# An adaLN block on one Trainium2 core: SyncE's transfers in the MLP phase in the order of the source, and several of them in other half steps

## The chip, the core and the metric

The kernel runs on one core of a Trainium2 chip (trn2). It is one program with one launch. The metric is the device time of one execution in microseconds (us); where several runs are told, their median is given. The profile is one profiled execution of the same program, with a time of its own.

The engines are named as the profile names them: PE is TensorE's matmuls and PEld its weight loads, DVE is VectorE, ACT is ScalarE, POOL is GpSimd and SP is SyncE. SP and POOL only start DMA transfers in the part of the kernel that matters here (POOL also does some small arithmetic of the layer norm); SPq and POOLq are their DMA queues.

## The reference

A conditioned transformer block over 2048 tokens (S) of 640 features (D), all in float32. The condition `c` gives six vectors of 640; the first half of the block is a linear attention, the second an MLP with squared ReLU.

```python
mod = (silu(c) @ w_mod).reshape(1, 6, 1, 640)
sa, ca, ga, sb, cb, gb = (mod[:, i] for i in range(6))
h = layernorm(x) * (1 + ca) + sa
x = x + ga * attention(h, wqkv, w_phi, wo)     # 32 heads of 20, hedgehog features (softmax of +p and -p)
h = layernorm(x) * (1 + cb) + sb
r = maximum(h @ w1 + b1, 0)                    # 640 -> 1728
x = x + gb * ((r * r) @ w2 + b2)               # 1728 -> 640
```

## The kernel before

**Products.** A float32 product is made of three products of a faster float32 form, fp32r. Each operand is split into `hi`, a rounded copy made by ACT, and `lo`, the difference to the original, made by DVE with one subtraction (`lo`, L88). `three` lists the three matmuls hi·hi, hi·lo and lo·hi, and `mm` (L78) issues all matmuls of the kernel, so all of them show L78 in the profile, and the tiles tell them apart.

**The MLP phase** begins near 409 us and is the part that the change touches. It works on 8 blocks `j` of 256 tokens (two tiles of 128). A block takes NP = 7 steps `n`, and each step has two half steps, `2n` and `2n+1`, one for each of the 14 chunks `f` of 128 hidden columns (the last chunk has 64). In a half step:

- `up(j, f)` multiplies the transposed and normalised tokens `h` by chunk f of w1 on PE (tile `up`); ACT adds b1 and takes the ReLU (L1149, tile `ft`), DVE squares it (L1150).
- After both chunks of a step, `split_a` splits the squares (hi on ACT at L1173, lo on DVE at L88, tiles `ra` or `rs`).
- One step later PE multiplies them by the chunks of w2 and adds up in the accumulators `acc` and `acc3x`. In blocks 0 and 1, and in the last step of every block, this is `down_plain`. From block 2 (the constant PLAIN) on it is `down_pair`, which takes a step's two chunks together as a 2 by 2 matrix product with seven products in place of eight. It needs sums and differences of the activations (`sums`, `split_s`, tile `rs`) and of the weights.

**The weight sums** are made once. For a pair n of w2's chunks, `t_load(n)` loads the rows again (tiles `traw`, L1213, SP), `t_sums(n)` builds the sums on DVE, and `t_split(n)` splits them into three pieces c, a and b (384, 384 and 256 columns) and stores them to DRAM (`td_c`, `td_a`, `td_b`, L1242, SP). From block 2 on, `t_fetch` (L1259) loads a piece from DRAM into one of the four buffers of the tag `ring` (`ring_c`, `ring_a`, `ring_b`), on POOL's queue, each when the piece four places ahead of it has been used. Pairs 0 to 4 are prepared in block 1 and stage their pieces in ring buffers; pair 5 (NP-2) is loaded at the end of block 1 (its loads start once pair 4 has freed buffers), is split in block 2 and stages its pieces in another tile, `tst_end`.

**The weights of the MLP.** 28 chunks (14 of w1, 14 of w2) are loaded and split into SBUF once, in the order of the list `preps`. The first ones are done before the MLP phase; in the MLP phase `prep(n)` does n chunks at the end of a half step: n copies on ACT (`p_hi`, L916), n subtractions on DVE (`p_lo`, L88), n loads on SP (`p_load`, L906 and L909). `PREPS` gives n for each half step of block 0: 0 and 4 by turns, and 0 and 1 in the sixth step.

**The next block's tokens.** While block j runs, `layer(j+1, at)` prepares block j+1 at half steps `at` from the tables LN_AT0 (block 1), LN_AT1 (block 2), LN_AT2 (block 3) and LN_AT (from block 4). `load_x1` loads the attention's result `xm` (from A1, L970) and the input rows `xx` (L971), four transfers of 320 KB; `add_x` adds them on DVE (L975) and stores the sum to X1 (L976); `ln_pieces` is the layer norm (ACT sums at L1383 and L1388, application at L1395); `t2` transposes on PE. Here "load", "add" and "ln" give the half step of each piece.

**The end of a block.** `residual(j)` loads the stored rows of X1 back (tiles `xr`, L1304, SP), `add_bias` adds b2 to them on DVE, the accumulators are emptied in the first half steps of the next block, and `finish` adds the residual and stores the rows to the output (`store`, L1311, SP).

**Buffers.** The rows pass through tags with few buffers: `s1` (5), `s2` (2), `ring` (4), `x0` (1, for xm). The weight rows of block 0, `traw`, `xr` and `xx` from block 3 on share `s1`; `xx` of blocks 1 and 2, the last weight rows and the rows `y` of the output share `s2`. A load waits until the last reader of its buffer is done.

**What sets the order.** The instructions of an engine run in a fixed order. Outside the MLP phase a planner orders them by costs of its own. In the MLP phase `tc.manual_schedule` keeps PE, DVE, ACT and POOL in the order of the source; SP isn't in its list, and so the planner places SP's transfers by its costs. In the main loop a half step is written as `up`, the splits and `down` of the step before, then what is prepared on the side:

```python
            if j < PLAIN:
                layer(j + 1, 2 * n)
            if 0 < m < NP - 2:
                t_split(m - 1)
            ...
            prep(next(PREPS, 0))
            if n == 0 and j:
                ...
            if n == (5, 5, 4, 3)[min(j, 3)]:
                residual(j)
```

Here `m = NP*j + n - NP - 1`, so m is -1 at the start of block 1 and counts steps from there.

Of the kernel before, what the change touches and what calls it, by code (L numbers as in the profile page):

```python
# [23 lines left out]
NF = 14  # L24
# [14 lines left out]
PLAIN = 2  # L39
# [12 lines left out]
def kernel(  # L52
# [54 lines left out]
    def tok2(tag, name, at=0, pool=None):  # L107

        bufs = 1
        if tag == "w":  # L110
            tag = f"w{next(w_at)}"
        elif pool is None:
            bufs = BUFS.get(tag, 1)
        t = (pool or mem).tile([P, 2 * D + (W2_AT if tag == 'late' else 128 if tag in W_LONG else 0)], F32, tag=tag, name=name, bufs=bufs)
        return t[:, at : at + 2 * D].rearrange("p (s d) -> p s d", s=2)

    def row(tag, name):
        return (pc if tag in ("s3", "s4") else mem).tile([P, D], F32, tag=tag, name=name, bufs=BUFS[tag])
# [75 lines left out]
    ET_ = mybir.EngineType  # L194
# [33 lines left out]
    for d in range(NC):  # L228
        if d % 2 == 0:
            both = tok2("w", f"rawv{d}")  # L230
# [419 lines left out]
    for t in range(2, NT - 2):  # L650
        j, i = divmod(t, 2)
# [276 lines left out]
    EARLY = 6  # L928
    preps = [("1", f) for f in range(EARLY)]
    preps += [("2", 0)]  # L930
    for f in range(NF):
        preps += [("2", f + 1)] * (f + 1 < NF) + [("1", EARLY + f)] * (EARLY + f < NF)
    assert len(preps) == 2 * NF
    places = []
    todo = {"load": list(preps), "hi": list(preps), "lo": list(preps)}
# [21 lines left out]
    XM, H2, R2 = {}, {}, {}  # L957

    XX = {}

    def load_x1(j):
        XM[j] = tok2("x0", f"xm{j}")
        if j:
            XX[j] = [row("s2" if j <= PLAIN else "s1", f"xx{j}_{i}") for i in range(2)]
        else:
            both = tok2("x1", "xx0")
            XX[j] = [both[:, i] for i in range(2)]
        for i in range(2):
            t = 2 * j + i
            nc.sync.dma_start(XM[j][:, i], A1[t])  # L970
            nc.sync.dma_start(XX[j][i], x[t * P : (t + 1) * P])  # L971

    def add_x(j, *tiles):
        for i in tiles:
            nc.vector.tensor_tensor(XM[j][:, i], XM[j][:, i], XX[j][i], op=ALU.add)  # L975
            nc.sync.dma_start(X1[j][:, i], XM[j][:, i])  # L976

    def t2(j, *ds):
        if 0 in ds:
            H2[j] = ht(f"h2_{j}", j, (0, 96))  # L980
        if j == 0:
            t_unit(XM[j], cols_b, H2[j], ds[0], f"b{j}", bank(f"tb{j}_{ds[0]}"))
            return
        p = tp(f"tb{j}_{ds[0]}")
        for k, d in enumerate(ds):
            t_in(XM[j], d, p[:, 256 * k : 256 * k + 256])
        for k, d in enumerate(ds):
            hf = p3.tile([P, 256], F32, tag="hf", name=f"hfb{j}_{d}")
            t_out(cols_b, H2[j], d, f"b{j}", p[:, 256 * k : 256 * k + 256], hf)
# [137 lines left out]
    NP = NF // 2  # L1127
# [29 lines left out]
    def plain(j, n):  # L1157
        return j < PLAIN or n == NF // 2 - 1 or j == NB - 1 and n >= NF // 2 - LAST
# [27 lines left out]
    def split_s(j, n):  # L1186
        t = FT[j, n]
        a = RS[j, n] = p3.tile([P, 2, 4, P], F32, tag="rs", name=f"rs{j}_{n}").bitcast(F32R)
        nc.scalar.activation(a[:, 0], t[:, S1 : S4 + 1], AF.Copy)
        lo(a[:, 1], t[:, S1 : S4 + 1], a[:, 0])  # L1190
# [18 lines left out]
    def t_load(n):  # L1209
        TR_[n] = [row("s1", f"traw{n}_{r}") for r in range(2)]  # L1210
        for r in range(2):
            f = 2 * n + r
            nc.sync.dma_start(TR_[n][r], w2[f * P : (f + 1) * P])  # L1213
# [92 lines left out]
    def add_bias(j, i):  # L1306
        add(XR[j, i], XR[j, i], bb)
# [61 lines left out]
    prev = None  # L1369
    LN2 = {}  # L1370

    LN_AT0 = {"load": 0, "add": (2, 4), "ln": (2, 4, 6, 6, 8, 8), 10: (0, 1), 11: (2, 3), 12: (4,)}
    LN_AT1 = {"load": 3, "add": (5, 5), "ln": (5, 6, 6, 7, 8, 8), 9: (0, 1), 11: (2, 3), 12: (4,)}
    LN_AT2 = {"load": 4, "add": (6, 6), "ln": (7, 7, 8, 8, 9, 9), 10: (0, 1), 11: (2, 3), 12: (4,)}
    LN_AT = {"load": 0, "add": (3, 4), "ln": (4, 5, 6, 6, 7, 7), 8: (0, 1), 10: (2, 3), 12: (4,)}
    PREPS = iter([0, 4] * 5 + [0, 1])

    def ln_pieces(xt, nm, spare):
        sm = small([P, 2], "sm", f"sm{nm}")
# [18 lines left out]
    def layer(j, at):  # L1398
        todo = {1: LN_AT0, PLAIN: LN_AT1, PLAIN + 1: LN_AT2}.get(j, LN_AT)
        if j == NB:  # L1400
            return
        if at in todo:
            t2(j, *todo[at])
        if todo["load"] == at:
            load_x1(j)
        for i in range(2):
            if todo["add"][i] == at:
                add_x(j, i)
        for i in range(6):
            if todo["ln"][i] == at:  # L1410
                if i == 0:
                    LN2[j] = ln_pieces(XM[j], f"b{j}", XX[j])
                next(LN2[j])

    by_hand = tc.manual_schedule(engines={ET_.PE, ET_.DVE, ET_.Activation, ET_.Pool})
    by_hand.__enter__()
    for j in range(NB):
        for n in range(NP):
            down = lambda k: prev and (down_plain if plain(*prev) else down_pair)(*prev, k)
            twice = not plain(j, n)  # L1420
            m = NP * j + n - NP - 1
            done = j - 1 if j and prev else None
            up(j, 2 * n)
            if prev and not plain(*prev):
                split_s(*prev)
            down(0)
# [4 lines that stand above are left out]
            if m == -1:  # L1431
                t_load(0)
            if (j, n) == (PLAIN, 0):
                t_fetch(4)
            if j >= PLAIN:
# [3 lines that stand above are left out]
                if j - 1 >= PLAIN:  # L1439
                    first_combos(j - 1)  # L1440
                else:
                    Y[j - 1] = [row("s2", f"y{j - 1}_{i}") for i in range(2)]
                for r, i, c in (("2", 0, L), ("3", 0, R)):
                    end(j - 1, r, i, c)
            if n == 1 and j:
                gate(j - 1, 0)
                if j != PLAIN:
                    finish(j - 1, j < PLAIN)
            if n == 1 and j == PLAIN:
                finish(j - 1, 0)  # L1450
            if n == 2 and j == PLAIN:
                t_sums(NP - 2)
            if n == (2 if j > PLAIN else 1) and j:
                gate(j - 1, 1)
            if n == (5, 5, 4, 3)[min(j, 3)]:
                residual(j)
            for i in range(2):
                if n == 6 and j == 0 or n == 5 and j >= PLAIN and i == 0:
                    add_bias(j, i)
            if j == NB - 1 and n == 1:  # L1460
                for k in range(NP - LAST, NP - 1):
                    plain_load(k)
            if j == NB - 1 and n == 3:
                for k in range(NP - LAST, NP - 1):
                    plain_split(k)
            if j == NB - 1 and n == NP - 2:
                for i in range(2):
                    by_gate(Y[j][i], Y[j][i], slice(0, D))
            if j == NB - 1 and n == NP - 1:
                split_a(j, n, (0,))  # L1470
                for i in range(2):
                    add(Y[j][i], Y[j][i], XR[j, i])
            up(j, 2 * n + 1)
            if j >= PLAIN and n == 0:
                down(1)
            split_a(j, n, (0, 1) if (j, n) != (NB - 1, NP - 1) else (1,))
            if twice:
                sums(j, n)
            if j < PLAIN or n:
                down(1)  # L1480
            if m == NP + 1:
                t_split(NP - 2)
            prep(next(PREPS, 0))
            if n == 0 and j:
                end(j - 1, "4", 1, L)
                end(j - 1, "x", 1, R)
            if n == (2 if j > PLAIN else 1 if j == PLAIN else 0) and j:
                finish(j - 1, j >= PLAIN)
            layer(j + 1, 2 * n + 1)
            if 0 <= m < NP - 2:  # L1490
                t_sums(m)
            if m == NP - 2:
                t_split(m - 1)
            if 0 < m + 1 < NP - 1:
                t_load(m + 1)
            if m == NP - 1:
                for i in range(2):
                    add_bias(j - 1, i)
            if j >= PLAIN and n == 5:
                add_bias(j, 1)  # L1500
            if j == NB - 1 and n == NP - LAST:
                first_combos(j)
            prev = j, n
# [61 lines left out]
```

## Time and profile before

| | |
|---|---|
| Runs | 801.79, 798.03 and 801.46 us |
| Median | 801.46 us |
| Profiled execution, its own time | 800.36 us |
| Its span in the profile | 798.7 us |
| Mean granted TensorE clock | 0.997 |
| DMA traffic | 126.30 MB, 158 GB/s over the span |

The span runs from the first to the last instruction of the profile; 800.36 - 798.7 = 1.7 us of the execution lie outside it. In the lists of groups and in the timelines, a row gives the start, the duration, the engine, the line, the operation and the tiles (out<-in), with "xcount" where several instructions of one kind follow each other; the idle time ahead of it and what ended that time stand in square brackets. A duration of several matmuls runs from the start of the first to the end of the last, and a weight load overlaps the matmul before it. In the table of stretches, the columns are the stretch, its length, the busy time of PE, PEld, DVE, ACT and POOL with the instruction counts, then the granted clock, the mean busy share of the DMA engines and GB/s.

### The profile page before, as it was taken

What the parts mean: (1) busy time and instruction counts of PE and PEld (TensorE: products, weight loads), DVE (VectorE), ACT (ScalarE), POOL (GpSimd) and SP (SyncE); (2) the same over time, 40 slices, a digit from 0 to 9 for tenths busy, and PEclk for the clock granted to TensorE, in tenths of its full rate; (3) what the DMA queues carried; (4) which work ended last, traced back from release to release, by engine and by line L of the source; (5) the groups of instructions that cost most, each with busy time, mean ns of one, the idle gap of its engine ahead of it and who ended that gap; (6) DMA issues with size and microseconds to landing.
All of it is one profiled execution on the core that took longest, in us unless ns stands there. A gap on an engine that the chain in (4) does not pass through costs nothing.

```text
span 798.7 us, 15281 instructions
## 1 busy us (share of the span) xinstructions
PE 785.4 (98%) x5983; PEld 750.5 (94%) x5983; DVE 579.3 (73%) x1046; ACT 443.3 (56%) x988; POOL 128.3 (16%) x259
## 2 busy tenths in 40 slices
PE   9999999999999999999999999998999999999997
PEld 8899999999999878898899999998999999999997
DVE  4499889998788688993546666775757667675756
ACT  4667675576753355565777737555364645536431
POOL 3001021010000114331000000131131313213110
PEclk9999999999999999999999999999999999999999
DMA  9713326423120243321347355996575967667450
GB/s 341 279 35 128 115 83 203 148 85 116 67 100 1 82 167 132 116 83 67 116 144 239 130 180 213 284 317 207 160 237 154 278 170 234 200 175 218 122 168 34
DMA packets 50560, 126.30 MB, mean 158 GB/s; under 512 B 5872, under 2 KB 6640, under 8 KB 50488
## 3 DMA queue, kind: packets, MB, share of 16 engines
q1 hardware_dynamic: 33432, 84.32, 31.0%
q0 software_dynamic: 14752, 35.76, 16.3%
q10 hardware_dynamic: 2304, 5.24, 1.7%
q8 instruction: 47, 0.77, 0.4%
q14 instruction: 25, 0.20, 0.1%
HBM read 95.32 MB, written 29.88 MB: 157 GB/s over the span
## 4 chain that ended last, share of the span: by engine, by line
PE 75%; DVE 10%; ACT 6%; issue 4%; POOL 3%; DMA 2%; POOLq 0%; ACTq 0%; DVEq 0%
PE up L78 18%; PE acc L78 14%; PE pk L78 8%; PE pq L78 7%; PE pv L78 7%; PE pwo L78 7%; PE acc3x L78 4%; PE kvp L421 2%; DVE dn L790 2%; DVE scr L788 2%; PE te L829 2%; DMA ring_b<-td_b 1%; PE ta L340 1%; PE tb L340 1%; DVE ezb L809 1%
## 5 line engine op out<-in xcount | busy, mean ns | idle before, releaser
L78 PE MATMUL up<-h,w 128*128 128x256 f32 x1640 | 208.7, 279 | 0.4 <-ACT ft L1149 0.4
L78 PEld LDWEIGHTS up<-h,w 128*128 128x128 f32 x1640 | 197.9, 189 | 1.1 <-ACT ft L1149 0.8
L1149 ACT ACTIVATE ft<-up,b_t 128x256 f32<-128x256 f32 x104 | 49.0, 472 | 106.6 <-PE up L78 106.1
L78 PE MATMUL acc<-w,ra 128*128 128x384 f32 x452 | 100.4, 338 | 0.4
L78 PE MATMUL pwo<-wo,ot 128*128 128x256 f32 (+3 forms) x512 | 83.2, 315 | 0.1
L1150 DVE TENSOR_TENSOR ft<-ft 128x256 f32<-128x256 f32 x104 | 44.0, 423 | 50.5 <-ACT ft L1149 48.8
L78 PE MATMUL pk<-wk,hT 128*128 128x384 f32 (+1 forms) x480 | 77.1, 312 | 0.9 <-ACT hT L352 0.9
L78 PEld LDWEIGHTS pwo<-wo,ot 128*128 128x128 f32 (+1 forms) x512 | 75.7, 188 | 1.9 <-ACT ot L866 0.4
L78 PEld LDWEIGHTS acc<-w,ra 128*128 128x128 f32 x452 | 72.7, 188 | 3.7 <-DVE ra L88 2.0
L78 PE MATMUL pq<-wq,hT 128*128 128x384 f32 (+1 forms) x480 | 74.9, 311 | 0.4 <-ACT k L397 0.4
L78 PE MATMUL pv<-wv,hT 128*128 128x384 f32 (+1 forms) x480 | 75.2, 309 | 0.0
L78 PEld LDWEIGHTS pk<-wk,hT 128*128 128x128 f32 x480 | 71.6, 188 | 2.7 <-ACT hT L352 1.1
L78 PEld LDWEIGHTS pq<-wq,hT 128*128 128x128 f32 x480 | 70.5, 188 | 1.5 <-ACT k L397 0.9
L78 PEld LDWEIGHTS pv<-wv,hT 128*128 128x128 f32 x480 | 70.5, 188 | 0.4
L88 DVE TENSOR_TENSOR ra<-ft,ra 128x384 fp32r<-128x384 f32 (+2 forms) x86 | 36.8, 449 | 34.3 <-ACT ra L1173 21.0
L88 DVE TENSOR_TENSOR h<-hfb,h 128x256 fp32r<-128x256 f32 x40 | 17.0, 425 | 46.4 <-ACT h L352 46.3
L1173 ACT ACTIVATE ra<-ft 128x384 fp32r<-128x384 f32 x48 | 25.2, 526 | 32.6 <-DVE ft L1150 25.2
L78 PE MATMUL acc3x<-w,ra 128*128 128x256 f32 x248 | 43.0, 281 | 0.0
L78 PEld LDWEIGHTS acc3x<-w,ra 128*128 128x128 f32 x248 | 39.5, 188 | 1.6 <-DVE y L1314 1.4
L1259 POOL DMA_DIRECT2D ring_a<-td_a x34 | 18.3, 540 | 129.9 <-PE acc L78 103.3
L792 POOL TENSOR_TENSOR dn<-dn,rs_q 128x64 f32<-128x64 f32 x16 | 14.0, 877 | 128.0 <-DVE dn L790 128.0
L1164 DVE TENSOR_TENSOR ft<-ft 128x128 f32<-128x128 f32 x136 | 33.3, 286 | 1.2
(241 smaller groups left out, 1424.5 us busy)
## 6 DMA issues: line engine op xcount, KB each, us to landing
ring_c<-td_c POOLq DMA_DIRECT2D x34, 384.0 KB, 4.6
ring_a<-td_a POOLq DMA_DIRECT2D x34, 384.0 KB, 4.2
ring_b<-td_b POOLq DMA_DIRECT2D x34, 256.0 KB, 4.5
esp<-eq SPq DMA_DIRECT2D x12, 640.0 KB, 3.0
el<-esp SPq DMA_DIRECT2D x12, 640.0 KB, 3.9
rw<-in_w SPq DMA_DIRECT2D x23, 320.0 KB, 3.1
wm<-in_w_mod SPq DMA_DIRECT2D x20, 320.0 KB, 3.8
xb<-in_x SPq DMA_DIRECT2D x8, 640.0 KB, 4.2
```

The costliest lines, as they stand in the source:

```text
L78: nc.tensor.matmul(o, a, b, start=first and i == 0, stop=last and i == len(terms) - 1, skip_group_check=skip,)
L88: (eng or nc.vector).tensor_tensor(out_lo, full, hi.bitcast(F32), op=ALU.subtract)
L340: nc.tensor.transpose(p[:, i * P : (i + 1) * P], xn[:, i, d * P : (d + 1) * P], ident)
L421: nc.tensor.matmul(kvp[64 * c : 64 * c + 64, g // 4, a : a + 2 * n].rearrange("p (s n) -> p s n", s=2), v[:, u], e[:, :, o : o + n], start ...
L788: nc.vector.tensor_tensor(z, flat(ET[t]), flat(zb), op=ALU.mult)
L790: nc.vector.tensor_reduce(dn.rearrange("p s h -> p (s h)"), heads(z), axis=AX.X, op=ALU.add)
L829: nc.tensor.transpose(p[:m, a : a + P], EU[2 * j + i][:, b : b + m], ident)
L1149: nc.scalar.activation(r, p, AF.Relu, bias=b1_t[:, f : f + 1])
L1150: nc.vector.tensor_tensor(r, r, r, op=ALU.mult)
L1164: nc.vector.tensor_tensor(t[:, o], t[:, a], t[:, b], op=op)
L1173: nc.scalar.activation(a[:, 0, :3], t[:, :3], AF.Copy)
L1259: nc.gpsimd.dma_start(RING[j, n, r], TD[n][r].bitcast(F32R))
```

## The change

- SP joins the list of engines that keep the order of the source in the MLP phase.
- `PREPS` becomes two weight chunks per half step, eleven times, and `preps` has the last chunk of w1 at its end.
- `load_x1` can load one of its two token tiles. LN_AT0 (block 1's tokens) loads them at half steps 1 and 2 in place of both at 0, adds them at 3 and 5 in place of 2 and 4, and begins the layer norm at 4 and 5 in place of 2 and 4; LN_AT, from block 4 on, loads them at 0 and 1 in place of both at 0. The other two tables keep their half steps.
- In block 2 the residual rows are loaded at step 5 in place of 4, and the bias is added at step 6 in place of 5.
- `t_split` of the last weight sums moves from step 2 to step 3 of block 2 (second half of the step).

```diff
     for f in range(NF):
-        preps += [("2", f + 1)] * (f + 1 < NF) + [("1", EARLY + f)] * (EARLY + f < NF)
+        preps += [("2", f + 1)] * (f + 1 < NF) + [("1", EARLY + f)] * (EARLY + f < NF - 1)
+    preps += [("1", NF - 1)]
...
-    def load_x1(j):
-        XM[j] = tok2("x0", f"xm{j}")
-        if j:
-            XX[j] = [row("s2" if j <= PLAIN else "s1", f"xx{j}_{i}") for i in range(2)]
-        else:
-            both = tok2("x1", "xx0")
-            XX[j] = [both[:, i] for i in range(2)]
-        for i in range(2):
+    def load_x1(j, tiles=(0, 1)):
+        if 0 in tiles:
+            XM[j] = tok2("x0", f"xm{j}")
...
+        for i in tiles:
             t = 2 * j + i
             nc.sync.dma_start(XM[j][:, i], A1[t])
             nc.sync.dma_start(XX[j][i], x[t * P : (t + 1) * P])
...
-    LN_AT0 = {"load": 0, "add": (2, 4), "ln": (2, 4, 6, 6, 8, 8), 10: (0, 1), 11: (2, 3), 12: (4,)}
-    LN_AT1 = {"load": 3, "add": (5, 5), "ln": (5, 6, 6, 7, 8, 8), 9: (0, 1), 11: (2, 3), 12: (4,)}
-    LN_AT2 = {"load": 4, "add": (6, 6), "ln": (7, 7, 8, 8, 9, 9), 10: (0, 1), 11: (2, 3), 12: (4,)}
-    LN_AT = {"load": 0, "add": (3, 4), "ln": (4, 5, 6, 6, 7, 7), 8: (0, 1), 10: (2, 3), 12: (4,)}
-    PREPS = iter([0, 4] * 5 + [0, 1])
+    LN_AT0 = {"load": (1, 2), "add": (3, 5), "ln": (4, 5, 6, 6, 8, 8), 10: (0, 1), 11: (2, 3), 12: (4,)}
+    LN_AT1 = {"load": (3, 3), "add": (5, 5), "ln": (5, 6, 6, 7, 8, 8), 9: (0, 1), 11: (2, 3), 12: (4,)}
+    LN_AT2 = {"load": (4, 4), "add": (6, 6), "ln": (7, 7, 8, 8, 9, 9), 10: (0, 1), 11: (2, 3), 12: (4,)}
+    LN_AT = {"load": (0, 1), "add": (3, 4), "ln": (4, 5, 6, 6, 7, 7), 8: (0, 1), 10: (2, 3), 12: (4,)}
+    PREPS = iter([2] * 11)
...
-        if todo["load"] == at:
-            load_x1(j)
+        for i in range(2):
+            if todo["load"][i] == at:
+                load_x1(j, (i,))
...
-    by_hand = tc.manual_schedule(engines={ET_.PE, ET_.DVE, ET_.Activation, ET_.Pool})
+    by_hand = tc.manual_schedule(engines={ET_.PE, ET_.DVE, ET_.Activation, ET_.Pool, ET_.SP})
...
-            if n == (5, 5, 4, 3)[min(j, 3)]:
+            if n == (5, 5, 5, 3)[min(j, 3)]:
                 residual(j)
             for i in range(2):
-                if n == 6 and j == 0 or n == 5 and j >= PLAIN and i == 0:
+                if n == 6 and j == 0 or n == (6 if j == PLAIN else 5) and j >= PLAIN and i == 0:
                     add_bias(j, i)
...
-            if m == NP + 1:
+            if m == NP + 2:
                 t_split(NP - 2)
...
-            if j >= PLAIN and n == 5:
+            if j >= PLAIN and n == (6 if j == PLAIN else 5):
                 add_bias(j, 1)
```

More of the change, by code (lines that the diff above doesn't have):

```diff
@@ L959 @@
     XX = {}
-    def load_x1(j):
-        XM[j] = tok2("x0", f"xm{j}")
-        if j:
-            XX[j] = [row("s2" if j <= PLAIN else "s1", f"xx{j}_{i}") for i in range(2)]
-        else:
-            both = tok2("x1", "xx0")
-            XX[j] = [both[:, i] for i in range(2)]
-        for i in range(2):
+    def load_x1(j, tiles=(0, 1)):
+        if 0 in tiles:
+            XM[j] = tok2("x0", f"xm{j}")
+            if j:
+                XX[j] = [row("s2" if j <= PLAIN else "s1", f"xx{j}_{i}") for i in range(2)]
+            else:
+                both = tok2("x1", "xx0")
+                XX[j] = [both[:, i] for i in range(2)]
+        for i in tiles:
             t = 2 * j + i
```

## The prediction

> **What bounds it now.** I read the page's busy times first, then the table of stretches, cut at the block starts of the MLP phase (block 0 starts at 409 us; 50 us or less each), then the waits.
>
> ```profile
> PE 785.4 (98%) x5983; PEld 750.5 (94%) x5983; DVE 579.3 (73%) x1046; ACT 443.3 (56%) x988; POOL 128.3 (16%) x259
> ```
> ```profile
> 505.00:552.00 47.00, 44.20 (x331) 43.46 (x330) 30.13 (x76) 22.27 (x49) 11.36 (x22) 0.96 0.86 272
> ...
> 599.00:645.00 46.00, 46.00 (x359) 45.35 (x358) 30.36 (x76) 24.04 (x51) 11.22 (x22) 1.00 0.71 210
> ...
> 785.00:799.00 14.00, 8.40 (x61) 7.91 (x59) 8.40 (x19) 1.88 (x5) 0.00 (x0) 0.94 0.13 47
> ```
>
> PE sets the time: in 599 to 645 it is never idle, so a smoother DMA queue has nothing to win in blocks 3 to 7. The last 14 us are stores behind DVE, which the change does not touch. What it can win lies in block 2 (505 to 552: 2.8 us idle, granted clock 0.96) and, by the waits below, in block 0. The first listing is PE's waits from 405 us on, the second those of the weight loads from 405 to 457.
>
> ```profile
> PE acc L78 <- DMA ring_b<-td_b: 2.2, 1, 2.2
> PE acc L78 <- DMA ring_a<-td_a: 0.6, 2, 0.3
> ```
> ```profile
> PEld acc L78 <- DVE w L88: 1.5, 4, 0.4
> ```
>
> The one large wait is for a transfer. The chain of waits shows how long that transfer took, PE's timeline what it did to PE, the stretches the clock behind it, and the DMA issues of 526 to 537.5 the other transfers of that time.
>
> ```profile
> 512.79 4.60 DMA ring_a<-td_a
> ...
> 531.69 9.47 DMA ring_b<-td_b
> ```
> ```profile
> 530.61 0.68 PE L78 MATMUL acc<-ring_a,rs 128*128 128x384 f32 x3
> ...
> 537.59 0.76 PE L78 MATMUL acc<-ring_a,rs 128*128 128x384 f32 x3 [0.32 <-DMA ring_a<-td_a]
> ...
> 541.20 1.01 PE L78 MATMUL acc<-ring_b,rs 128*128 128x256 f32 x3 [2.17 <-DMA ring_b<-td_b]
> ```
> ```profile
> 537.80:541.20 3.40, 1.23 (x9) 1.03 (x8) 1.88 (x6) 1.00 (x2) 1.04 (x3) 1.00 1.12 393
> 541.20:544.60 3.40, 3.40 (x16) 3.40 (x17) 0.00 (x0) 1.37 (x2) 0.53 (x1) 0.50 0.85 265
> ```
> ```profile
> xr<-x SPq DMA_DIRECT2D x2, 320.0 KB, 8.2
> ```
>
> The fetch issued at 531.69 had 541.20 - 2.17 - 531.69 = 7.3 us until PE wanted it, and took 9.5. The residual rows beside it took 8.2: stores of the last weight sums, residual rows, stored x rows and the next block's x rows stood in the DMA engines together. After the wait the clock was at half for 3.4 us.
>
> **The change, part by part.** The base is the profiled execution: 800.36 us, 798.7 of them span. The median of the runs is 801.46.
>
> *Block 2's crowd.* The residual loads go from step 4 to 5, the sums' stores one step later, the next block's x rows out of the crowd. With it go 2.17 + 0.32 of waiting and half of 3.4 us of clock: **-4.2**; if a crowd remains that still takes 8 us, nothing. [...]
>
> *Bias additions a half step later in block 2.* They stood between the split and the square of the steps that also transpose. From PE's timeline, the last step of block 2 and of block 3:
>
> ```profile
> 550.57 2.01 PE L78 MATMUL up<-h,w 128*128 128x256 f32 x15
> ...
> 558.20 1.93 PE L78 MATMUL up<-h,w 128*128 128x256 f32 x15
> ...
> 598.33 1.98 PE L78 MATMUL up<-h,w 128*128 128x256 f32 x15
> ...
> 604.89 1.30 PE L78 MATMUL up<-h,w 128*128 128x256 f32 x10
> ```
>
> 7.63 against 6.56 us, with the same matmuls: **-1.1** (0 to -1.1).
>
> *Weights, two per half step.* Half of them are split a half step earlier, so the four waits for w go: **-1.5**. The price is at the start and in the middle of block 0.
>
> At the start, two copies and two subtractions now stand before the second square. DVE, ACT and PE there, and in the middle:
>
> ```profile
> 413.53 0.42 DVE L1150 TENSOR_TENSOR ft<-ft 128x256 f32<-128x256 f32 x1 [0.25 <-ACT ft L1149]
> ...
> 429.79 3.03 DVE L88 TENSOR_TENSOR w<-rw,w 128x640 fp32r<-128x640 f32 x4
> ```
> ```profile
> 427.46 0.46 ACT L1149 ACTIVATE ft<-up,b_t 128x256 f32<-128x256 f32 x1
> ...
> 429.04 2.61 ACT L916 ACTIVATE w<-rw 128x640 fp32r<-128x640 f32 x4
> 431.55 0.46 ACT L1149 ACTIVATE ft<-up,b_t 128x256 f32<-128x256 f32 x1
> 431.91 0.82 ACT L1388 ACTIVATE xx<-xm,smb 128x640 f32<-128x640 f32 x1
> ...
> 433.53 0.46 ACT L1149 ACTIVATE ft<-up,b_t 128x256 f32<-128x256 f32 x1
> 434.49 0.53 ACT L1173 ACTIVATE ra<-ft 128x384 fp32r<-128x384 f32 x1 [0.50 <-DVE ft L1150]
> ```
> ```profile
> 414.57 1.04 PE L78 MATMUL acc<-w,ra 128*128 128x384 f32 x3
> ...
> 436.59 0.68 PE L78 MATMUL acc<-w,ra 128*128 128x384 f32 x3
> ```
> ```profile
> L975 DVE TENSOR_TENSOR xm<-xm,xx 128x640 f32<-128x640 f32 x2 | 1.6, 818 | 0.0
> L1383 ACT ACTIVATE xx<-xm 128x640 f32<-128x640 f32 x2 | 1.5, 740 | 3.9 <-DVE xm L975 3.9
> ```
>
> A subtraction takes 3.03 / 4 = 0.76. DVE was idle for 0.25 before 413.53, so two of them push that square by 1.3, and the split that PE took at 414.57 with it: **+1.2** (0.6 to 1.3).
>
> In the middle, the second x tile is added in half step 5 instead of 4, behind that half step's subtractions, and ACT's sum over it stands before the next relu. Subtractions from 429.79 end at 431.31, the addition (0.82) at 432.13, the sum (0.74) at 432.87. The relu that began at 431.55 begins 1.3 later. Then the two squared sums follow as before, and now two weight copies (2.61 / 2 = 1.3) before the relu of half step 7, which begins 2.6 later, at 436.2. Its split with the subtraction was ready near 434.49 + 0.53 + 0.56 = 435.6 (the last half of a 0.76-to-0.82 subtraction pair, my estimate) and was wanted at 436.59: 1.0 of cover. PE waits **+1.6** (0.5 if DVE and ACT run ahead there; 2.4 if the weight loads come late, since four x loads now stand between them on SP, which before went out ahead of them).
>
> *SP in the order of the source.* The loads of the last weight sums' rows (t_load(5)) stand before the stores of t_split(4) in the source, and need the slots which that split frees. Before, SP's queue was:
>
> ```profile
> 507.91 0.33 SPq L1213 DMA_DIRECT2D traw<-in_w  x1
> 508.29 0.43 SPq L1242 DMA_DIRECT2D td_a<-tst_a  x1
> ...
> 509.29 0.66 SPq L1213 DMA_DIRECT2D traw<-in_w  x1
> ```
>
> Now td_a stands behind the second load: 509.29 + 0.66 - 508.29 = 1.7 later. The fetch at 512.79 waits for the slot that td_a's landing frees, and PE already waited 0.3 for it. **+0.5** (-0.3, if the x loads that no longer run at 503 to 508 speed it up; +1.7 in full); nearer the middle, as the queue before it is emptier. POOL's later fetches queue behind, with 3 us and more of room.
>
> *The last weight split a step later.* Four ACT copies move to a half step that has two layer-norm sums:
>
> ```profile
> 525.71 0.51 ACT L1239 ACTIVATE tst_end<-traw 128x384 fp32r<-128x384 f32 x1
> ```
> ```profile
> 535.13 0.69 DVE L88 TENSOR_TENSOR rs<-ft,rs 128x512 fp32r<-128x512 f32 x1
> ```
>
> Four of at most 0.51 delay the split that ended at 535.82 and was wanted at 537.59 - 0.32: 1.4 of cover against some 1.5 to 2. **+0.2** (0 to 1.1).
>
> *Block 3's x rows.* They go out together, after the second output store near 521.4, instead of at 503, 518 and 521; three of the four 320 KB loads are now ahead of the fetch below. POOL's timeline, the DMA issues of 518 to 527, and the rates:
>
> ```profile
> 522.97 0.54 POOL L1259 DMA_DIRECT2D ring_a<-td_a  x1 [2.69 <-PE acc L78]
> ```
> ```profile
> ring_a<-td_a POOLq DMA_DIRECT2D x1, 384.0 KB, 4.5
> ```
> ```profile
> 518.00:526.00 8.00, 8.00 (x66) 8.00 (x65) 5.71 (x16) 2.72 (x6) 2.17 (x4) 1.00 1.06 354
> ...
> 532.00:536.00 4.00, 4.00 (x33) 4.00 (x32) 2.57 (x7) 3.64 (x10) 1.01 (x4) 1.00 0.85 215
> ```
>
> It landed at 527.5 and PE wanted it at 530.61: 3.1 of room. 0.98 MB more ahead cost 2.8 at 354 GB/s, 4.6 at 215. **+0.4** (0 to 4), near the lower end because the stretch itself ran at 354. [...]
>
> In blocks 3 to 7 PE waits for none of what moves: nothing. Sum: -4.2 - 1.1 - 1.5 + 1.2 + 1.6 + 0.5 + 0.2 + 0.4 = -2.9, 797.5 against 800.36. The runs' median is 1.1 above the profiled execution and I do not know which of them the next runs follow, so I put half of it on: **798.0**.
>
> **Rivals.**
>
> *No new waits.* ACT and DVE catch up in block 0 and every fetch lands in time: -4.2 - 1.1 - 1.5 + 0.6 - 0.3 = -6.5, with the 0.55 some 794.4. For it: ACT is 56% busy, and both queues were idle at times in block 0. Against: the sum for half step 7 is a plain in-order chain.
>
> *The crowd only moves; slower.* From 521 on three more loads stand before the fetches of block 2's third step. Below 0.98 MB / 3.1 us = 316 GB/s PE waits again; at 215 by 1.5. The sums' stores and the residual, now together near 535 to 538, then cost a second wait like today's 2.5, td_a its full 1.7, and each of the two crowds a half-clock window of 1.7: -4.2 - 1.1 - 1.5 + 1.2 + 1.6 + 0.2 + 1.7 + 1.5 + 2.5 + 3.4 = +5.3, 805.7, on the runs' footing 806.2. For it: the 215 row stood in just such a crowd. Against: bytes per us are fewer than at 526 to 537.
>
> *Nothing changes.* If SP's order comes out nearly as it was and the crowd is a matter of chance in each run: 800.4 to 801.5.
>
> **How the numbers follow.** Forecast 0.48 (its own range 796.5 to 800.5), no new waits 0.24, crowd moves 0.20, nothing 0.08. About 0.5% (4.0 us of 801.46) is what a measurement of this kernel can tell from no change: below 797.45 is faster, above 805.47 slower. Faster: all of the second, 0.10 of the first: 0.34. Slower: 0.14 of the third, the rest of it being half its price. Within: 0.52. The range 794.5 to 804.0 leaves out about a tenth on each side.
>
> **What would show it.** Right: no wait for ring_b near 541 and no clock of 0.50 there; a wait of PE for ra near 436 to 439; no PEld wait for w in block 0; td_a after both traw loads, the first ring_a later than 512.79; xm and xx of block 3 issued together near 522. Wrong: waits of PE for ring tiles between 530 and 547, or no wait for ra in block 0, or PE waiting in blocks 3 to 7.

## The result and the profile after

The changed kernel takes 800.08 us (median of 22 runs), the kernel before 797.70 us (median of 22 runs beside them). The ratio is 1.0021 with a 95% interval of 1.0011 to 1.0031: slower by 0.2%, or about 1.7 us (the two medians alone lie 2.4 us apart, 0.3%). The prediction was 798.0, against a profiled execution of 800.36 and a median of 801.46 for the kernel before, so a small gain. The result lies inside its range and inside what it called no change, but on the other side of its sign.

Two things came out of the comparison before any experiment. First, two of the three runs shown before the prediction (median 801.46) and the profiled execution (800.36) were high ones: the median of the 22 is 797.70. Second, in the profiles the change does two opposite things. A block is counted here from its first `up` matmul to that of the next block, in PE's timeline. Of the changed kernel, the starts of blocks 0, 1 and 2 are:

```profile
409.50 5.65 PE L78 MATMUL up<-h,w 128*128 128x256 f32 x45
...
461.73 1.86 PE L78 MATMUL up<-h,w 128*128 128x256 f32 x15
...
510.28 1.86 PE L78 MATMUL up<-h,w 128*128 128x256 f32 x15
...
559.66 1.99 PE L78 MATMUL up<-h,w 128*128 128x256 f32 x15
```

The last row is block 3's start. Read in the same way, the kernel before has 409.06, 457.04, 505.57 and 558.20. Block 0 went from 47.98 to 52.23 us (+4.25), block 1 from 48.53 to 48.55, block 2 from 52.63 to 49.38 (-3.25). Block 0 also starts 0.44 later. The sum, +1.46, is the difference of the spans (800.1 against 798.7). Blocks 3 to 6 take 46.5 to 46.7 us in both, so LN_AT's later load of the second tile costs and wins nothing there. PE's waits in the MLP phase, and the stretches of blocks 0, 2 and 3, show the same:

```profile
PE acc L78 <- ACT ra L1175: 3.4, 3, 1.9
PE up L78 <- ACT ft L1151: 1.2, 1, 1.2
PE acc L78 <- DMA ring_a<-td_a: 0.8, 1, 0.8
```
```profile
405.00:457.00 52.00, 48.49 (x359) 46.78 (x358) 31.60 (x57) 35.79 (x73) 2.14 (x5) 0.97 0.54 178
505.00:552.00 47.00, 45.08 (x344) 43.73 (x343) 31.94 (x81) 24.56 (x56) 10.72 (x21) 1.00 0.88 280
552.00:599.00 47.00, 47.00 (x366) 46.16 (x365) 31.81 (x77) 25.24 (x56) 11.28 (x22) 1.00 0.68 208
```

PE's wait for ring_b and the weight loads' waits for w are gone, as forecast. In their place PE waits for the split activations `ra` (three times, all in block 0), once for a ReLU (`ft`) and once for ring_a, both in block 2. In the stretch of 505 to 552 the granted clock is 1.00 where it was 0.96; now it is block 0's that is low, 0.97.

What happens in block 0 is read from four timelines. SP, from 409 us on, and one row of SP's waits for the same stretch:

```profile
414.48 0.33 SPq L906 DMA_DIRECT2D rw<-in_w  x1
...
418.53 0.83 SPq L909 DMA_DIRECT2D rw<-in_w  x1
419.46 0.37 SPq L972 DMA_DIRECT2D xm<-a  x1
419.94 0.37 SPq L973 DMA_DIRECT2D xx<-in_x  x1
```
```profile
SPq L906 <- DVE w L88: 24.7, 2, 22.5
```

SP stood at the first weight load until a subtraction on DVE freed its buffer, and the x rows of block 1 stood behind it. Four weight loads, two of half step 0 and two of half step 1, were ahead of them (414.48, 415.22, 417.80 and 418.53); the first row went out at 419.46. In the kernel before, the planner had put rows of block 1 ahead of block 0's weight rows:

```profile
408.31 0.80 SPq L970 DMA_DIRECT2D xm<-a  x2
413.06 0.33 SPq L971 DMA_DIRECT2D xx<-in_x  x1
416.23 0.33 SPq L906 DMA_DIRECT2D rw<-in_w  x1
```

DVE, ACT and PE of the changed kernel after that:

```profile
426.09 0.83 DVE L977 TENSOR_TENSOR xm<-xm,xx 128x640 f32<-128x640 f32 x1 [2.05 <-DMA xx<-in_x]
...
433.23 0.82 DVE L977 TENSOR_TENSOR xm<-xm,xx 128x640 f32<-128x640 f32 x1
```
```profile
434.09 0.74 ACT L1385 ACTIVATE xx<-xm 128x640 f32<-128x640 f32 x1 [1.74 <-DVE xm L977]
...
436.90 1.35 ACT L916 ACTIVATE w<-rw 128x640 fp32r<-128x640 f32 x2
438.15 0.45 ACT L1151 ACTIVATE ft<-up,b_t 128x256 f32<-128x256 f32 x1
439.58 0.52 ACT L1175 ACTIVATE ra<-ft 128x384 fp32r<-128x384 f32 x1 [0.98 <-DVE ft L1152]
```
```profile
416.14 1.04 PE L78 MATMUL acc<-w,ra 128*128 128x384 f32 x3 [0.98 <-ACT ra L1175]
...
430.95 1.03 PE L78 MATMUL acc<-w,ra 128*128 128x384 f32 x3 [0.59 <-ACT ra L1175]
...
440.16 1.03 PE L78 MATMUL acc<-w,ra 128*128 128x384 f32 x3 [1.85 <-ACT ra L1175]
...
442.57 3.14 PE L78 MATMUL up<-h,w 128*128 128x256 f32 x15
```

DVE waits 2.05 us for the row, with the square of the next half step behind it. The delay goes from queue to queue, DVE's addition, ACT's sum and copies, ReLU, square, split, and PE waits 0.59 and then 1.85 us. Each of these waits cost PE more than its idle time: the first three matmuls behind it took 1.03 or 1.04 us together (the rows above) in place of the 0.68 of those that did not wait. What a late operand costs in all is read from `up` to `up`, 3.42 us for a half step in which nothing is late; the half steps of the waits near 431 and 440 take 4.52 and 6.13. The `up` at 442.57 takes 3.14 us instead of the usual 1.86: the clock is at half for 3.4 us, which this stretch shows (granted clock in the third column from the end):

```profile
441.80:445.20 3.40, 3.40 (x18) 3.40 (x17) 2.06 (x4) 3.00 (x5) 0.00 (x0) 0.50 0.90 263
```

In block 2 the crowd in the DMA engines is still there. It no longer holds a ring fetch that PE wants at once, but the last x row of block 3. DMA issues of 527.8 to 528.1, then DVE and PE:

```profile
xx<-in_x SPq DMA_DIRECT2D x1, 320.0 KB, 9.3
```
```profile
537.21 0.83 DVE L977 TENSOR_TENSOR xm<-xm,xx 128x640 f32<-128x640 f32 x1 [1.96 <-DMA xx<-in_x]
```
```profile
522.65 0.76 PE L78 MATMUL acc<-ring_a,rs 128*128 128x384 f32 x3 [0.76 <-DMA ring_a<-td_a]
...
542.23 1.99 PE L78 MATMUL up<-h,w 128*128 128x256 f32 x15 [1.16 <-ACT ft L1151]
```

### The profile page after: what moved, and what is told of

It reads as the page before. It is cut to its first block, busy times and chain, and to the rows that moved or that the text cites. A ratio compares the mean times of both kernels' runs of the same rounds, so it can differ in the third digit from the quotient of the medians.

```text
span 800.1 us, 15269 instructions
## 1 busy us (share of the span) xinstructions
PE 784.9 (98%) x5983; PEld 750.2 (94%) x5983; DVE 580.4 (73%) x1046; ACT 443.0 (55%) x988; POOL 128.5 (16%) x259
## 4 chain that ended last, share of the span: by engine, by line
PE 79%; DVE 9%; ACT 4%; DMA 3%; POOL 2%; issue 1%; SPq 1%; ACTq 0%; DVEq 0%; POOLq 0%
PE up L78 20%; PE acc L78 15%; PE pk L78 8%; PE pq L78 7%; PE pv L78 7%; PE pwo L78 7%; PE acc3x L78 5%; PE kvp L421 2%; DMA xx<-in_x 2%; DVE dn L790 2%; DVE scr L788 2%; PE te L829 2%; PE tb L340 1%; DMA xb<-in_x 1%; PE ta L340 1%
## 5 line engine op out<-in xcount | busy, mean ns | idle before, releaser
L449 DVE TENSOR_REDUCE rs_q<-eq 128x64 f32<-128x1280 f32 x16 | 23.5, 1472 | 14.8 <-ACT eq L408 14.8
```

The source lines that it names most:

```text
L449: nc.vector.tensor_reduce(s, heads(flat(e)), axis=AX.X, op=ALU.add)
```

## The experiments

Theory A: block 0's loss comes from the order in the queues, of two kinds: x rows that stand on SP behind weight loads, and copies, subtractions, additions and sums that stand on ACT and DVE ahead of ReLU and square. Block 2's moves are a real gain. The rivals were that only one of the two kinds matters, or that block 2's gain was nothing but the one bad execution that had been profiled. All medians and ratios, and the blocks of each profile (us). Each ratio is to runs of the kernel before made beside that run (median 798.08 for e1 to e4, 798.45 for e5 to e8, 798.13 for e9 to e11); e7 and e8 have 5 runs, e2 has 6, the others 11 or 12.

| Run | Edit | Median | Ratio to before, 95% | Block 0 | Block 2 |
|---|---|---|---|---|---|
| e1 | before, unchanged | 797.88 | 1.0004 (0.9993 to 1.0016) | 47.25 | 49.81 |
| e2 | changed, block 0's part undone | 795.75 | 0.9973 (0.9962 to 0.9984) | 47.15 | 48.02 |
| e3 | changed, SP to the planner | 796.26 | 0.9975 (0.9963 to 0.9987) | 48.50 | 47.34 |
| e4 | before, SP in source order | 796.91 | 0.9980 (0.9971 to 0.9990) | 47.17 | 48.57 |
| e5 | changed, x rows loaded first | 796.92 | 0.9978 (0.9967 to 0.9988) | 48.55 | 48.02 |
| e6 | changed, PREPS undone | 797.88 | 0.9993 (0.9984 to 1.0002) | 49.19 | 48.19 |
| e7 | before, block 2's moves | 795.06 | 0.9962 (0.9950 to 0.9975) | 47.16 | 47.30 |
| e8 | e2, td stores first | 794.73 | 0.9957 (0.9945 to 0.9969) | 47.21 | 47.75 |
| e9 | e8, xm rows early | 795.27 | 0.9969 (0.9948 to 0.9991) | 47.07 | 46.89 |
| e10 | changed, unchanged | 799.60 | 1.0018 (1.0007 to 1.0029) | 49.96 | 48.78 |
| e11 | changed, LN_AT0 undone | 797.00 | 0.9983 (0.9973 to 0.9992) | 48.39 | 49.96 |

**e1, the kernel before once more.** No edit.

> The kernel before, unchanged. In the first profile of before, the wait for ring_b (2.2 us) and the half clock behind it stood in a transfer that took 9.5 us. Theory A (that transfer is a matter of chance, most executions of before don't have it): ratio 1.000, median 797 to 798, and the profile shows block 2 (first matmul of its first half step to that of block 3) in 48.5 to 50 us instead of 52.6, without a half clock near 541. Theory B (it is a fixed property of before's order, and the lower median comes from elsewhere): block 2 takes 52 to 53 us again and the wait for ring_b is there.

Neither theory quite. Block 2 took 49.81 us, not 52.6, without the half clock; but the wait for ring_b was there again, behind a fetch of 8.5 us:

```profile
540.93 0.63 PE L78 MATMUL acc<-ring_b,rs 128*128 128x256 f32 x3 [1.77 <-DMA ring_b<-td_b]
```

So the wait belongs to before's order, its size varies, and the half clock after it came in one of the two profiles. The ratio 1.0004 shows what the comparison makes of two equal kernels.

**e2, block 0's part undone.** From the changed kernel:

```diff
-    preps += [("1", NF - 1)]          # and the guard back to EARLY + f < NF
-    LN_AT0 = {"load": (1, 2), "add": (3, 5), "ln": (4, 5, 6, 6, 8, 8), ...
-    PREPS = iter([2] * 11)
+    LN_AT0 = {"load": (0, 0), "add": (2, 4), "ln": (2, 4, 6, 6, 8, 8), ...
+    PREPS = iter([0, 4] * 5 + [0, 1])
```

> The changed kernel with block 0's part undone: PREPS, the order of preps, and LN_AT0 as before; SP stays in the order of the source, block 2's moves stay. Theory A (the 4.3 us that block 0 lost come from ACT's and DVE's order: copies, subtractions, x additions and sums ahead of ReLU and square): block 0 takes 48 us instead of 52.2, the waits for ra at 416, 431 and 440 are gone, no half clock there; 800.1 - 4.2 = 796 us. Theory B (SP's order is to blame: x rows land late behind weight rows): block 0 keeps at least half of the loss, 798 to 800 us.

Theory A's number: 795.75, block 0 at 47.15. The rest of the change, SP's order and block 2's moves, is faster than before by 0.27%. All of the loss needs block 0's part, but it doesn't come from that part alone, as e3 shows. Since the edit also puts the x loads back to half step 0, it can't tell theory A's cause from theory B's.

**e3, SP left to the planner.** From the changed kernel:

```diff
-    by_hand = tc.manual_schedule(engines={ET_.PE, ET_.DVE, ET_.Activation, ET_.Pool, ET_.SP})
+    by_hand = tc.manual_schedule(engines={ET_.PE, ET_.DVE, ET_.Activation, ET_.Pool})
```

> The changed kernel with SP's order left to the planner again; all other parts of the change stay. Theory A (ACT's and DVE's order makes block 0's loss): block 0 still takes 51 to 52.5 us; 799 to 800.5 us. Theory B (SP's order makes it): block 0 takes 48 to 49 us, 796 to 797 us.

Theory B's number: block 0 at 48.50, 796.26 us. With the planner's order the wait of 0.98 near 416 stayed, that near 438 fell to 0.84, the half clock was gone. So block 0's part costs 1.3 us of block 0 by itself (48.50 against e2's 47.15), SP's order nothing there (e4 has it alone), and together they cost 2.8 to 5.1 (e10 and the first profile of the changed kernel).

**e4, SP's order alone**, the reverse of that line in the kernel before.

> The kernel before with one line of the change: SP in the order of the source. PREPS, LN_AT0 and block 2's moves as before. Theory A (SP's order alone costs nothing in block 0, and td_a behind the second traw load costs 0.4 us in block 2): 797.5 to 798.5 us, block 0 at 48 us, a wait of 0.3 to 0.8 us for the first ring_a of block 2. Theory B (SP's order is the loss): 799.5 to 801 us, block 0 at 50 us or more.

Block 0 is untouched (47.17), and the price of td_a behind the second traw load is there, 0.88 us:

```profile
518.51 0.76 PE L78 MATMUL acc<-ring_a,rs 128*128 128x384 f32 x3 [0.88 <-DMA ring_a<-td_a]
```

But the kernel is faster, not slower: 0.9980. In the order of the source the residual rows stand behind the stores of x, and so leave the crowd by themselves; that this is the gain is read from one execution of each. SP of e1, then of e4, and the ring_b fetch that had 8.5 us in e1, in e4's DMA issues of 532.5 to 533:

```profile
529.92 2.04 SPq L1304 DMA_DIRECT2D xr<-x  x2
532.05 0.99 SPq L976 DMA_DIRECT2D x<-xm  x2
```
```profile
531.64 2.12 SPq L976 DMA_DIRECT2D x<-xm  x2
533.82 1.03 SPq L1304 DMA_DIRECT2D xr<-x  x2
```
```profile
ring_b<-td_b POOLq DMA_DIRECT2D x1, 256.0 KB, 6.0
```

**e5, the x rows first.** From the changed kernel, one entry:

```diff
-    LN_AT0 = {"load": (1, 2), "add": (3, 5), ...
+    LN_AT0 = {"load": (0, 0), "add": (3, 5), ...
```

> The changed kernel with one edit: LN_AT0 loads both x tiles of block 1 at half step 0 instead of 1 and 2, so that on SP they stand ahead of block 0's weight rows; additions, sums, PREPS and the rest stay. Theory A (most of block 0's loss is that the x rows stood on SP behind weight loads that wait for a buffer: issued at 419.5 instead of 409, landed at 426, and DVE's queue stood behind the addition): block 0 takes 48.3 to 49 us instead of 52.2, the wait of 1.0 us near 416 stays, no half clock near 440; 796 to 797 us. Theory B (the loss lies in the places of copies, additions and sums on ACT and DVE, whenever the rows come): block 0 stays at 51 us or more, 799 us or more.

Theory A: 796.92 us, block 0 at 48.55. The intervals of e5 (0.9967 to 0.9988) and of the changed kernel (1.0011 to 1.0031) lie apart; 1.0021 - 0.9978 = 0.43%, 3.4 us for the place of the loads of two tiles. In the profiles, block 0 loses 3.7 us against e5 in the first one of the changed kernel, with a half clock, and 1.4 in e10, without. They differ in block 2 as well (49.38 and 48.78 against 48.02), and whether that hangs on these loads isn't shown. SP, DVE and PE of e5:

```profile
409.06 0.33 SPq L972 DMA_DIRECT2D xm<-a  x1
409.55 0.33 SPq L973 DMA_DIRECT2D xx<-in_x  x1
```
```profile
424.25 0.82 DVE L977 TENSOR_TENSOR xm<-xm,xx 128x640 f32<-128x640 f32 x1
```
```profile
416.39 1.04 PE L78 MATMUL acc<-w,ra 128*128 128x384 f32 x3 [0.98 <-ACT ra L1175]
...
438.32 1.04 PE L78 MATMUL acc<-w,ra 128*128 128x384 f32 x3 [0.87 <-ACT ra L1175]
```

The first tile's rows leave 10 us earlier, the addition runs without a wait, the wait of 0.59 is gone and that of 1.85 is 0.87.

**e6, PREPS and preps as before**, LN_AT0 of the change.

> The changed kernel with PREPS and preps as before (0 and 4 weight chunks by turns); LN_AT0 with its loads at half steps 1 and 2, SP's order and block 2's moves stay. Theory A (x rows behind weight loads): four weight loads now stand ahead of the first x tile, so the rows are late again: issued after 418, block 0 at 49.5 to 52 us; the wait of 1.0 us near 416 is gone (0.1 to 0.2 as before). Theory B (two weights per half step are the loss, by their place on ACT and DVE): block 0 at 47 to 48 us, 796 us.

Between the two: the x rows are late again (issued at 420.40) and PE waits 1.07 us for `ra` near 438.6, without half clock; block 0 takes 49.19, just under A's bounds. Against e2, late rows without two weights per half step cost 49.19 - 47.15 = 2.0 us of block 0, two weights without late rows 48.55 - 47.15 = 1.4 (e5); both have LN_AT0's later additions and sums. PREPS and the order of `preps` were only undone together. Neither edit is harmless without the other, so theory B's 796 is wrong here, and so is a theory A that names SP alone.

**e7, block 2's moves alone**, in the kernel before:

```diff
-            if n == (5, 5, 4, 3)[min(j, 3)]:
+            if n == (5, 5, 5, 3)[min(j, 3)]:
                 residual(j)
-            if m == NP + 1:
+            if m == NP + 2:
                 t_split(NP - 2)          # and the two places of add_bias
```

> The kernel before with block 2's moves alone: residual at step 5, its bias at step 6, the last split a step later; SP's order left to the planner, block 0 as before. Theory A (these moves take the residual rows and sums out of the stretch in which the ring fetches stood, and that is a real gain in a typical execution too): block 2 takes 47.3 to 48 us against 49.8 in the second profile of before, no wait for ring_b near 541, 795.0 to 796.0 us. Theory B (only the odd execution with the half clock loses anything, so the moves are worth nothing in the median): 797 to 798 us.

Theory A: 795.06 us, 0.38% faster, block 2 at 47.30, and PE idle for 0.11 us in the whole stretch:

```profile
505.00:552.00 47.00, 46.89 (x361) 45.95 (x360) 33.39 (x86) 25.84 (x58) 11.69 (x23) 1.00 0.90 287
```

**e8, the td stores first**, on top of e2:

```diff
             if m == NP - 2:
                 t_split(m - 1)
-            if 0 < m + 1 < NP - 1:
+                t_load(m)
+            if 0 < m + 1 < NP - 2:
                 t_load(m + 1)
```

> The run e2 (the change without block 0's part) with one more edit: on SP the loads of the last weight sums' rows go behind the stores of the split before them. Theory A (td_a behind the second traw load makes the wait for ring_a of 0.6 to 0.9 us at the start of block 2): that wait goes, block 2 from 48.0 to 47.4 us, 795.1 us. Theory B (ring_a is late for the four fetches on POOL that start together, whatever SP's order): the wait stays at 0.5 us or more, 795.7 us.

The wait at the first ring_a (0.6 in e2) is gone, so it was SP's order. (In e2 the profile puts it down to DVE's addition to `y`, which ended at 517.89, about when the fetch landed. It wasn't that: in e8 the same matmul starts at 516.56, before that addition ends at 517.30.) Block 2 took 47.75 rather than 47.4, because in this execution the ring_b fetch of 530.65 took 7.5 us and PE waited 0.5 for it. The median, 794.73, is the lowest of all, 0.43% under before.

**e9, block 3's xm rows early**, on top of e8: loaded at the first half step of block 2, the xx rows where they were.

> The run e8 (block 0's part undone, td_a ahead of the traw loads) with one more edit: block 3's two xm rows are loaded at the first half step of block 2, as the planner had them, instead of with the xx rows near 521. Theory A (each 320 KB that leaves the stretch from 521 to 545 shortens the transfers in it): the wait of 0.5 us for ring_b near 538 in e8 goes, ring_b's slowest transfer falls from 7.5 to about 6 us, block 2 takes 47.3 us, 794.3 us. Theory B (the early rows delay traw and td_a instead): a wait for ring_a near 517 of 0.3 us or more, 794.7 to 795.5 us.

The profile is theory A's: no wait of PE between 418 and 600 us, ring_b at 5.5 us, block 2 at 46.89, the shortest of all. The median (795.27) is not: one of its 12 runs took 803.9 and its interval reaches 0.9991. e7, e8 and e9 can't be told apart by their times; each is faster than both kernels.

**e10, the changed kernel once more.**

> The changed kernel, unchanged. Theory A (block 0's loss is fixed by the order of queues, block 2's wait for x rows is partly chance): ratio 1.002 against before, block 0 at 51 to 52.5 us with a wait of 1.5 us or more for ra near 440; block 2 between 48 and 49.5 us. Theory B (block 0's loss with its half clock is chance too): block 0 at 50 us or less in this profile.

The wait is fixed, the half clock is not. PE waited the same 1.85 us, and the `up` behind it ran at full speed:

```profile
439.74 1.03 PE L78 MATMUL acc<-w,ra 128*128 128x384 f32 x3 [1.85 <-ACT ra L1175]
...
441.85 1.87 PE L78 MATMUL up<-h,w 128*128 128x256 f32 x15
```

Block 0 took 49.96, outside A's bounds: without the half clock (half of 3.4 us), and without the wait of 0.59, since the first xx row came 1 us earlier (the half step near 431 takes 3.87 us, that near 440 takes 5.82). The ratio, 1.0018, repeats the first.

**e11, LN_AT0 as before, two weights per half step kept.**

> The changed kernel with LN_AT0 as before (loads at half step 0, additions at 2 and 4, sums from 2 on); PREPS stays at two per half step, SP's order and block 2's moves stay. Theory A (of block 0's 1.4 us in e5, 0.85 are the start, where two copies and two subtractions stand ahead of the second square, and 0.85 the later places of addition and sums): the wait of 1.0 us near 416 stays, that of 0.9 us near 438 goes; block 0 at 47.8 us, 796.2 us. Theory B (the wait near 438 comes from the weight copies ahead of the ReLU, wherever the sums stand): it stays at 0.6 us or more; block 0 at 48.4 us, 796.9 us.

By the waits theory A: 1.00 at 416 stays, 0.87 near 438 is gone. By block 0's time (48.39) theory B. The half steps show why the two don't agree. The one near 438 takes 3.42 us, 1.4 less than in e5. But those that begin at 421.50 and 428.98 take 4.06 and 4.04 in place of 3.42, 1.3 more together, though PE is idle for only 0.11 and 0.10 us in them: their split `ra` came late on ACT. It seems that, with two weights per half step, the earlier additions and sums only move the loss to other half steps. No gain of e11 over e5 shows in the medians; its profiled execution (798.28) was the slowest of its 12, with an xx row of 10.2 us in block 2.

## Why the prediction was right or wrong

**The step that failed: where the x rows stand on SP.** The prediction saw that in block 0 x loads and weight loads now share one order, and costed it as weights behind x rows ("2.4 if the weight loads come late"). It is the other way round. LN_AT0 moved the x loads from half step 0 to 1 and 2, four weight loads that wait for a buffer came ahead of them, and the first rows went out 10 us later than in e5. That is 3.4 us (e5) which no term of the sum held. Without it the change comes out at 796.9, faster by 0.22%.

**The base was mis-sized.** The sum was made against a profiled execution with a wait of 2.17 us and a half clock. Other executions of the same kernel have less: 49.81 us for block 2 in e1 instead of 52.63. The saving there was forecast as -4.2 and -1.1, with +0.2 for the split: -5.1. Against the first profile e7 measures 47.30 - 52.63 = -5.3, against e1 -2.5, and in the ratio -0.38%, 3.0 us. The mechanism was right; what it is worth in the median is little more than half. Of the parts, the bias additions can be read by themselves: block 2's last step takes 7.63 and 7.60 us in the two profiles of before and 6.76 in e7, -0.9 for the forecast -1.1.

**Weight waits, -1.5:** right, though PE's idle time hides it. In block 0 of before, PE is idle for only 0.14, 0.10, 0.08 and 0.12 us at the four late weights, but the matmuls behind them run late too. From `up` to `up`, the first of these half steps of before takes 3.80 us, the next, without a late weight, 3.42:

```profile
420.47 1.86 PE L78 MATMUL up<-h,w 128*128 128x256 f32 x15
...
423.03 1.05 PE L78 MATMUL acc<-w,ra 128*128 128x384 f32 x3
...
424.27 1.86 PE L78 MATMUL up<-h,w 128*128 128x256 f32 x15
...
427.69 1.86 PE L78 MATMUL up<-h,w 128*128 128x256 f32 x15
```

Read in this way, the four late weights of before cost some 1.5 us. e2 has three, whose weight loads wait 1.0 us in all, and they cost PE 1.1; e5 and the changed kernel have none:

```profile
PEld acc L78 <- DVE w L88: 1.0, 3, 0.4
```

**Start of block 0, +1.2:** counted from block 0's start, the first `acc` matmul of the phase comes at 416.39 - 409.76 = 6.63 us in e5 and at 415.49 - 409.96 = 5.53 in e2, +1.1, within 0.6 to 1.3. **Middle of block 0, +1.6:** the chain of addition, sum, copies, ReLU, square and split is the one that the prediction wrote down, and PE waits where it said (near 438 to 440). With the rows in time its half step takes 4.84 us in e5 in place of 3.42, +1.4; late rows add to that 0.45 us near 431 and 1.0 near 440 (e10), or 1.1 and 2.6 with the half clock (changed kernel). The three terms were forecast at +1.3 together. In e5 they come to -1.1 + 1.1 + 1.4 = +1.4, which is 48.55 - 47.15: each was about right, and what block 0 lost beyond them came with the late rows.

**td_a behind the second traw load, +0.5:** right: waits of 0.6 (e2) to 1.23 us (e11) in all profiles with SP in the order of the source but e8 and e9, against 0.32 and none in the two profiles of before; e8's one edit removes it. **The split a step later and block 3's x rows, +0.2 and +0.4:** the rows were late, but the price didn't go through a ring fetch. It went through DVE's addition and ACT's sums and copies into one ReLU. Counted from block 2's first `up`, the last xx row landed after 25.5 us in e2 and e5, 26.3 in e10, 26.9 in the changed kernel and 27.5 in e11, and PE waited 0.25, 0.15, 0.79, 1.16 and 1.16 us for that ReLU; in e3, where the planner placed the rows, not at all. It seems to take both moves: in e4 the row landed after 26.6 us, but the last split was at its old place, and PE didn't wait there. The prediction also put the bytes of the x rows ahead of POOL's fetch. No run shows such an order between the two queues: the traces show that both were slow at once, the fetch with 9.47 us beside transfers of 8.2, and a shared rate would look the same.

**SP's order by itself** was costed at +0.9 and gained 0.2% (e4): the prediction moved the residual for block 2's part and didn't see that the new order alone moves it behind the stores of x as well.

**The rivals.** "The crowd only moves" named the sign and half the mechanism, the x rows of block 3, but its price was put on ring fetches of block 2's third step, for which PE didn't wait; the loss lay in block 0, which it left as forecast. "No new waits" (794.4) is about what e7 and e8 are, at 795.1 and 794.7, with block 0's part left out.

## What to carry to other kernels

When a queue goes from a planner's order to the order of the source, list for each transfer what stands ahead of it and what that waits for: a load without a reason to wait, put behind one that waits for a buffer, is as late as the buffer (here the x rows, issued at 419.46 us in the changed kernel and at 409.06 in e5). Two cheap edits can meet there, so undo each alone and both. And before a wait in one profiled execution is booked as a saving, look at a second execution; the same fetch in a crowd was not equally late each time (9.47 us and a wait of 2.17, then 8.50 and 1.77 in e1). What a wait costs is read from the distance between equal steps, since an engine's idle time alone can hide most of it (0.44 us of idle time for some 1.5 us at before's four late weights).

## What the runs showed of the hardware

An idle gap of PE near 1.8 us was followed by the half clock in one execution and not in others: 1.85 us was in the changed kernel (3.4 us at 0.50, as after the 2.17 us of before), and the same 1.85 us was not in e10, nor 1.77 us in e1; none of 1.23 us or less was. It makes the price of one wait differ by 1.7 us, half of the 3.4, between executions of one program. How often it comes can be estimated from the mean granted clock of each run. The two profiles with it have 0.997 (before) and 0.996 (changed), the eleven others 0.998 to 1.000. 3.4 us at half clock lower the mean by 0.002, and so, at most, does the half clock at the end of these two profiles (0.56 over the last 1.7 us of before, 0.89 over the last 15.1 us of the changed kernel). So a mean of 0.997 or less is counted here as one that has it. By that estimate it stands in 14 of the 34 runs of the changed kernel (10 of 22, and 4 of 12 in e10), in one of e9 (the 803.9 us), in 5 to 9 of the 23 to 30 runs of before in each group, and in none of the 74 runs of e2 to e8 and e11, whose profiles have no gap of over 1.23 us.

What decides it in one execution was not shown. The length of the gap alone doesn't, as 1.85 us came with it and without it. In before the clock fell as the gap ended (541.20 us), in the changed kernel 1.6 us later (the gap ended at 440.16 us, the clock was 1.00 until 441.78).

The two forms of float32 matmul differ in the profile of before: those of 128x512 in fp32r took 394 ns (L864, numb<-ot,neg, median of eight), those of 128x480 in plain float32 618 ns (L734, z<-kvs,ident, mean of two).
